# A local-attention, mixture-of-experts and gated-convolution kernel whose planner gets another table of due times and another table of engine choices

## The chip, the cores and the metric

The kernel runs on one core of a Trainium2 chip, as one launch. The metric is the device time of that launch in microseconds (us). Before the change it is 360.0 us, the median of 3 runs (359.75 to 361.68). The engines are named as the profile names them: PE (TensorE, matrix products and transposes), DVE (VectorE), ACT (ScalarE), POOL (GpSimd) and SP (SyncE, which issues the transfers).

## The reference, cut to what matters

B = 4 batches, H = 8 heads of D = 64, S = 576 positions, 512 model columns.

```
# 1. local attention, per batch and head
q_d, k_d, v_d = means over groups of 4 positions           # 144 positions
out_d    = softmax(q_d k_d^T / 8) v_d, repeated 4 times
scores   = q k^T / 8, and -1e9 where |i - j| >= 4
attn_out = out_d + softmax(scores) v                        # -> x: (B, S, 512)
# 2. mixture of 4 experts, head width 64, the best 2 per token
w = softmax over the 2 best of x w_gate
out = sum over e in best 2 of  w_e * (causal_softmax((x wq_e)(x wk_e)^T / 8) (x wv_e)) wo_e
# 3. gated causal convolution, 5 taps, on x = out
gate_pre[t] = sum_k conv_w[k] * x[t + k - 4];  gate = 1 / (1 + exp(-gate_pre))
result = (gate * (x w_val)) w_out
```

## The kernel before, in words

Batches follow each other, and the attention of the next batch is worked on beside the experts and the convolution of the present one. Heads go in pairs, 128 rows at a time.

*Attention.* Queries and keys arrive as 128 x 576 (two heads of 64 rows); the pair sums L941 and L948 make the pooled queries qd and keys kd, and L965 and L971 the pooled values vd. L1072 makes the pooled scores. The band scores are taken over query windows of 58 positions against 64 keys: L1131 puts the mask into a PSUM bank, L1137 adds the products. A softmax is a chain of pieces: the maximum L1002 (DVE), the factor L1008, the exponential, the sum, the small constant L1042 or L1044, the reciprocal L1048 (DVE) and the normalisation. The exponential has forms. L1013 is one ACT instruction per row group that also sums (a READ of its accumulator follows it in the trace); L1019 is the same without the sum, which L1033 or L1035 then does on DVE; L1024 and L1028 subtract on DVE and take all exponentials in one ACT instruction. The normalisation is L1057 on ACT (one instruction per row group, five for p, three for pd) or L1059 on DVE or POOL (one for all). PE transposes the weights (L1088 pooled, L1150 band), ACT or DVE copies them out of PSUM (L1095, L1157), PE multiplies with the values (L1106, L1172), and L1181 and L1189 make the 512 columns of x, which L793 and L810 split into a high and a low part.

*Weights.* They come as 8-byte numbers and are decoded by a chain of three ACT, POOL and DVE pieces with DVE's L858, L862 and L870; then they are split into high and low parts too. L891 multiplies the expert output weights with w_val. Products of split numbers are three matmuls, L1217 to L1219.

*Experts.* Projections by L1217 to L1219 (xh, xl with wqk; wvg makes values and gate), causal scores L1369, a softmax against a running maximum of scores (L1396, L1399, L1408 on ACT with sums), the gate's weight by L1509, transposes L1430 and L1447 (the fifth, last query tile of each pair of experts is L1447's), copies L785, and the products with the values L1541.

*Convolution and output.* wo and wv products again by L1217 to L1219; five taps, one with L1589 or L1596 on ACT and the others as L1603 on DVE, L1601 on POOL; L1608 is the tanh that stands for the sigmoid, L1614 the gate product, then the product with w_out, its scale L1635 or L1637, and the output's DMA L1641.

*What sets the order.* No instruction's place is written out by hand. The code builds `pieces`: some instructions of one engine with a cost, the buffers they read and write, and a due time. `order()` then plays the engines through in time: whenever an engine is free, of the pieces whose inputs are there and for which buffers are free (8 PSUM banks, two to six slots of each kind in SBUF) the one with the earliest due time is taken. The order so found is recorded, and the chip follows it on each engine, with semaphores between engines. Two tables feed it. `DUE` has one number for each piece (line 34 on), used in the line

```
p = Piece(engine, cost, late, (DUE[idx] if idx < len(DUE) else 0.0, idx), fn, k, size)
```

and `PICK` (line 254 on) has one digit for each choice that `pick(name, *options)` offers: which engine does a piece, or which form a softmax takes.

```
k = min(int(PICK[n]), len(options) - 1) if n < len(PICK) else 0
```

The rest of the file, below the tables, is this:

Of the kernel before, what the change touches and what calls it, by code (L numbers as in the profile page):

```python
# [34 lines left out]
    0.3, 0.5, 0.7, 3.85, 0.6, 0, 0.15, 3.6, 5.16, 4.91, 4.66, 0.9, 4.89, 0, 1.9, 5.41, 1, 0.5, 6.63,  # L35
    17.11, 6.13, 5.43, 6.16, 4.13, 5.94, 1.5, 2, 10.6, 25.96, 11.1, 6.27, 7.22, 7.34, 8.15, 18.43,
    20.51, 8.74, 10.69, 11.4, 11.74, 11.74, 13.08, 14.95, 16.34, 16.63, 11.2, 12.56, 13.48, 13.03,
    13.03, 15.15, 15.91, 17.43, 21.16, 22.44, 22.86, 23.49, 24.63, 27.11, 12.78, 14.43, 15.12, 15.59,
    15.58, 15.03, 15.03, 17.03, 18.05, 19.32, 19.54, 14.83, 15.43, 16.61, 15.9, 15.43, 15.43, 15.9,
    21.69, 22.83, 23.12, 24.4, 25.14, 25.74, 26.3, 27.38, 28.37, 29.43, 30.14, 27.38, 28.07, 31.01,  # L40
    31.52, 19.75, 21.9, 22.7, 23.34, 23.03, 22.5, 22.5, 23.03, 26.08, 29.26, 29.82, 22.3, 23.27, 23.74,
    26.08, 22.9, 22.9, 27.67, 28.27, 29.35, 29.66, 31.23, 31.97, 32.31, 32.87, 34.08, 34.96, 35.63,
    36.3, 34.08, 34.65, 35.24, 35.9, 17.61, 16.61, 30.21, 29.21, 31.71, 25.32, 26.64, 22.05, 23.27,
    21.39, 21.89, 29.71, 37.9, 36.9, 28.27, 29.02, 28.8, 29.44, 40.34, 42.55, 25.43, 26.88, 28.07,
    28.41, 28.41, 27.47, 27.47, 29.75, 30.82, 33.8, 34.26, 27.27, 27.87, 34.8, 28.34, 27.87, 27.87,
    28.34, 36.89, 37.7, 39.84, 29.95, 32.07, 32.78, 33.47, 33.47, 33.47, 36.74, 37.61, 37.92, 31.55,
    32.27, 32.61, 32.65, 35.38, 36.67, 37.52, 37.81, 39.55, 41.17, 40.65, 43.5, 45.55, 45.59, 41.88,
    42.94, 43.53, 45.32, 46.91, 47.84, 49.15, 49.64, 46.91, 46.91, 48.73, 50.53, 35.16, 36.73, 37.32,
    38.83, 37.66, 37.32, 37.32, 37.66, 42.32, 43.44, 43.96, 37.12, 37.72, 37.72, 37.72, 43.04, 43.64,
    44.5, 45.8, 46.06, 46.28, 48.1, 49.09, 49.61, 50.92, 51.93, 52.32, 52.95, 53.56, 51.93, 52.02,  # L50
    52.52, 53.15, 0, 3.77, 5.09, 4, 11.72, 12.4, 5.63, 14.81, 16, 3, 8.93, 9.43, 25.46, 31.3, 32.58,
    2.5, 8.32, 9.19, 18.11, 25.21, 26.79, 10.1, 16.43, 18.58, 1.6, 5.49, 4.8, 5.26, 5.03, 4.5, 3.5,
    10.69, 12.93, 12.05, 12.73, 13.71, 15.23, 16.11, 18.03, 5, 16.11, 20.41, 20.97, 21.19, 22.92, 24.05,
    25.57, 28.34, 27.15, 30.71, 28.71, 37.37, 36.81, 39.49, 40.24, 42.7, 44.9, 50.06, 48.86, 49.33,
    67.4, 71.57, 72.12, 72.74, 73.46, 74.01, 75.39, 78.04, 76.3, 79.23, 0, 80.02, 78.73, 0, 79.42,
    22.39, 30.95, 33.18, 28.21, 34.42, 37.79, 86.78, 92.73, 93.33, 93.14, 94.05, 97.11, 97.75, 98.07,
    98.12, 102.59, 103.62, 103.54, 104.39, 105.05, 106.89, 107.89, 108.63, 45.79, 53.97, 54.52, 54.88,
    55.81, 56.56, 58.16, 60.05, 62.54, 59.05, 63.22, 63.77, 63.99, 64.46, 65, 66.51, 67.46, 70.02,
    76.28, 80.78, 81.33, 82.34, 83.11, 83.9, 85.82, 86.81, 88.53, 58.91, 59.28, 59.64, 64.32, 65.01,
    64.91, 62.41, 62.87, 63.23, 63.6, 64.32, 64.59, 58.55, 60.88, 61.24, 63.96, 66.52, 64.8, 32.28,  # L60
    36.5, 53.1, 55.98, 57.01, 56.95, 53.65, 54.02, 54.38, 55.18, 57.27, 56.82, 68.36, 69.12, 65.52,
    69.46, 70.55, 71.62, 65.34, 66.33, 75.39, 75.72, 76.66, 77.25, 77.83, 78.14, 82.54, 89.2, 67.25,
    68.93, 69.29, 69.64, 70.23, 70.77, 66.8, 67.61, 68.48, 70.86, 72.41, 71.54, 73.13, 72.64, 73.44,
    74.58, 75.04, 75.95, 77.49, 64.68, 65.03, 65.39, 65.74, 66.78, 66.33, 68.81, 33.85, 37.07, 51.7,
    54.74, 57.26, 57.83, 55.41, 58.94, 57.02, 57.59, 71.31, 71.75, 72.2, 73, 73.81, 73.67, 74.33, 57.23,
    57.67, 58.11, 60.44, 61.77, 62.26, 61.55, 62.59, 61.11, 62.83, 55.54, 56.34, 56.78, 60, 60.67,
    60.67, 61.35, 5.93, 6.04, 73.79, 75.08, 75.61, 74.81, 76.22, 76.25, 76.91, 76.85, 78.27, 78.95,
    79.29, 79.56, 82.47, 79.56, 81.57, 79.56, 82.08, 79.56, 80.16, 85.84, 87.63, 87.08, 89.02, 92.07,
    91.37, 94.15, 95.99, 95.66, 79.51, 80.89, 81.95, 80.62, 82.37, 84.37, 85.62, 83.45, 86.36, 89.99,
    90.49, 90.76, 92.04, 90.76, 91.34, 90.76, 90.95, 91.57, 91.97, 92.6, 93.84, 93.47, 94.43, 95.73,  # L70
    95.49, 97.41, 102.01, 97.92, 87.91, 89.29, 90.25, 89.89, 90.81, 93.22, 93.98, 94.25, 94.84, 94.89,
    95.22, 96.2, 97, 99.88, 91.1, 92.4, 94.21, 94.15, 96.33, 97.81, 98.25, 98.52, 98.52, 98.52, 99.86,
    100.99, 103.14, 102.11, 91.98, 95.26, 93.61, 96.41, 98.17, 99.4, 98.92, 100.1, 100.58, 100.85,
    102.54, 103.76, 105.19, 105.82, 106.67, 109.23, 109.23, 109.77, 109, 110.83, 111.63, 112.46, 113.98,
    114.76, 115.1, 115.39, 116.83, 115.3, 116.32, 118.2, 118.93, 120.22, 118.7, 120.68, 121.72, 122.18,
    123.23, 124.36, 125.31, 125.6, 126.47, 125.58, 125.7, 129.07, 129.93, 129.93, 119.4, 122.92, 121.82,
    124.29, 125.23, 125.99, 125.51, 127.78, 128.09, 128.37, 128.81, 130.3, 131.05, 130.94, 132.65,
    135.21, 135.21, 135.89, 31.21, 26.47, 43.74, 59.55, 68.4, 42.02, 44.23, 33.89, 38.39, 36.4, 37.4,
    43.24, 63.64, 67.9, 45.03, 46.3, 47.08, 47.98, 51.16, 52.22, 46.68, 49.21, 49.81, 49.81, 49.81,
    50.04, 50.64, 52.75, 55.68, 56.92, 58.86, 48.81, 49.41, 49.41, 49.41, 50.44, 51.03, 53.45, 54.45,  # L80
    55.23, 56.16, 52.24, 53.85, 55.08, 55.62, 55.55, 55.55, 58.02, 58.85, 59.31, 54.37, 55.08, 57.54,
    55.52, 55.52, 59.19, 59.95, 60.25, 66.1, 67.2, 67.05, 75.39, 76.56, 76.73, 67.97, 69.72, 69.73,
    77.26, 78.27, 78.77, 79.71, 80.68, 78.27, 78.47, 79.15, 79.53, 61.6, 63.07, 63.78, 64.64, 64.12,
    63.67, 63.67, 64.12, 68.23, 68.72, 69.14, 63.47, 64.07, 64.62, 68.71, 64.07, 64.07, 70.15, 71.26,
    71.8, 72.09, 79, 80.09, 80.44, 81.01, 81.92, 82.68, 83.31, 85.14, 81.92, 82.04, 86.07, 88.5, 48.83,
    48.33, 53.33, 86, 79.55, 58.22, 60.04, 55.32, 55.88, 63.14, 62.64, 53.83, 98.62, 85.5, 67.23, 67.99,
    67.72, 68.63, 60.75, 77.43, 70, 71.89, 72.92, 74, 73.42, 73.42, 75.53, 76.16, 77.36, 71.1, 71.82,
    72.67, 72.16, 72.16, 75.32, 76.08, 76.36, 81.69, 83.86, 85.17, 86.55, 89.71, 90.96, 80.2, 81.24,
    81.88, 82.35, 82.71, 81.84, 81.84, 84.77, 85.69, 86.58, 87.33, 81.64, 82.3, 83.74, 82.77, 82.24,
    82.24, 82.77, 86.03, 87.54, 88.52, 90.46, 91.63, 92.88, 93.44, 94.88, 98.75, 100.61, 101.65, 96.09,  # L90
    98.07, 100.64, 101.02, 83.96, 86.68, 87.28, 87.28, 87.28, 88.1, 89.89, 90.56, 96.28, 96.78, 97.37,
    88.8, 89.4, 89.4, 89.4, 91.67, 92.37, 93.22, 94.99, 95.57, 96.28, 106.16, 106.9, 107.24, 109.63,
    110.64, 113.06, 114.61, 115.21, 110.64, 111.1, 111.73, 112.11, 95.84, 97.95, 98.56, 98.54, 99.14,
    98.54, 99.66, 98.54, 100.18, 98.54, 100.71, 101.35, 100.28, 100.64, 102.02, 103.38, 103.78, 97.59,
    99.92, 101.66, 100.51, 102.75, 100.51, 104, 104.83, 106.29, 100.99, 107.13, 108.72, 104.19, 104.65,
    109.4, 109.93, 110.5, 97.22, 99.12, 104.48, 99.71, 105.18, 99.71, 105.7, 99.71, 106.49, 99.71,
    107.69, 108.41, 105.44, 105.8, 109.07, 109.6, 110.17, 96.7, 98.76, 100.25, 99.35, 101.1, 99.35,
    101.62, 99.35, 102.35, 99.35, 103.14, 104.17, 102.6, 103.4, 104.85, 105.51, 106.1, 114.82, 115.53,
    115.89, 116.68, 117.31, 138.94, 111.17, 111.62, 111.98, 112.33, 113.49, 119.94, 112.69, 113.04,
    113.4, 115.18, 117.4, 117.89, 121.06, 122.57, 123.4, 126.24, 127.08, 139.44, 136.6, 139.13, 139.89,  # L100
    139.81, 140.95, 139.81, 141.87, 139.81, 142.53, 139.81, 143.12, 143.78, 147.01, 150.58, 151.5,
    152.1, 152.9, 139.57, 141.55, 144.5, 148.26, 148.89, 147.03, 149.72, 142.23, 150.85, 142.23, 151.9,
    152.56, 154.09, 154.63, 156.18, 156.79, 157.26, 122.12, 137.51, 138.19, 138.19, 140.49, 138.19,
# [1598 lines left out]
```

## Time and profile before

| what | value |
|---|---|
| median of 3 runs | 360.0 us (359.75 to 361.68) |
| the profiled execution's own time | 360.29 us |
| its span, first to last instruction | 358.6 us |
| mean granted clock of PE | 0.986 of full speed |
| busy: PE | 331.2 us (92%) |
| busy: DVE, ACT, POOL | 301.5, 257.8, 197.5 us (84%, 72%, 55%) |
| moved by DMA | 31.70 MB, mean 88 GB/s |

The span lies inside the profiled execution's time; 1.7 us are around it. Busy time is the time in which at least one instruction of the engine was under way. Shares are averages over the whole span, and the stages of this kernel differ, so the table of stretches further down says more than they do.

### The profile page before, as it was taken

The page shows a single profiled execution, that of the slowest core. Times are in us where ns is not written, and L with a number is a line of the kernel's source. Part 1 is how long each engine was busy: PE and PEld are TensorE (multiplying, and loading weights), DVE is VectorE, ACT ScalarE, POOL GpSimd, SP SyncE. Part 2 cuts the span into 40 slices and gives each one's busy share as a digit, 9 for nine tenths or more (in the row PEclk, how much of TensorE's full clock was granted, in tenths as well). Part 3 has the DMA queues.
Part 4 walks back from the last instruction along what each step waited for, and adds up shares of the span by engine and source line. Part 5 has one row for each costly group of instructions (what it writes and reads, how often), then busy time and mean ns, then how long its engine had stood idle before and what let it go on. Part 6 is the DMA issues. An engine that isn't in the chain of part 4 may idle for free.

```text
span 358.6 us, 11498 instructions
## 1 busy us (share of the span) xinstructions
PE 331.2 (92%) x4360; PEld 290.1 (81%) x4360; DVE 301.5 (84%) x922; ACT 257.8 (72%) x893; POOL 197.5 (55%) x309
## 2 busy tenths in 40 slices
PE   0598499898899999999999999999999999999996
PEld 0465379886587998999899898999989899987896
DVE  5789999989999799999998876867889678599481
ACT  2769546789997977888888799577964473588372
POOL 6697768569987243579877221663751024017151
PEclk9999679999999999999999999999999999999999
DMA  7879774437450224325512100022000000010012
GB/s 257 214 262 239 176 211 132 141 99 158 122 160 3 72 64 136 97 81 148 133 43 69 53 31 1 2 78 76 2 1 3 31 15 16 18 59 2 15 46 74
DMA packets 26279, 31.70 MB, mean 88 GB/s; under 512 B 2672, under 2 KB 18032, under 8 KB 26224
## 3 DMA queue, kind: packets, MB, share of 16 engines
q1 hardware_dynamic: 26224, 30.97, 30.2%
q8 instruction: 34, 0.56, 0.7%
q14 instruction: 21, 0.17, 0.2%
HBM read 26.24 MB, written 4.72 MB: 86 GB/s over the span
## 4 chain that ended last, share of the span: by engine, by line
PE 75%; DVE 16%; ACT 3%; POOL 1%; DMA 1%; issue 1%; SPq 0%; DVEq 0%; ACTq 0%; POOLq 0%
PE ps L1217 18%; PE ps L1218 15%; PE ps L1219 15%; PE ps L1541 6%; PE ps L1369 5%; PE ps L1430 3%; PE ps L1172 3%; DVE mx L1002 2%; PE ps L1150 2%; PE ps L1106 2%; PE ps L1137 2%; PE ps L1072 2%; DMA kt<-in_kT_dram 1%; PE ps L891 1%; DVE o L858 1%
## 5 line engine op out<-in xcount | busy, mean ns | idle before, releaser
L1408 ACT ACTIVATE pe<-ps,mmin 128x128 f32<-128x128 f32 (+4 forms) x80 | 42.1, 532 | 13.8 <-DVE mmin L1399 6.8
L1603 DVE SCALAR_TENSOR_TENSOR row<-ps,cw,row 128x256 f32<-128x256 f32 (+1 forms) x94 | 45.7, 510 | 5.4 <-POOL row L1601 2.7
L1601 POOL TENSOR_TENSOR row<-row,row 128x320 f32<-128x320 f32 (+1 forms) x34 | 28.5, 840 | 32.8 <-ACT row L1589 18.5
L1217 PE MATMUL ps<-gh,wout_h 128*128 128x256 f32 (+1 forms) x128 | 39.1, 306 | 0.0
L1217 PE MATMUL ps<-xh,wqk_h 128*128 128x256 f32 (+1 forms) x128 | 38.7, 302 | 0.4 <-ACT pd L1019 0.4
L1218 PE MATMUL ps<-gl,wout_h 128*128 128x256 f32 (+1 forms) x128 | 37.7, 295 | 0.0
L1218 PE MATMUL ps<-xl,wqk_h 128*128 128x256 f32 (+1 forms) x128 | 37.7, 295 | 0.0
L1219 PE MATMUL ps<-gh,wout_l 128*128 128x256 f32 (+1 forms) x128 | 37.7, 294 | 0.0
L1219 PE MATMUL ps<-xh,wqk_l 128*128 128x256 f32 (+1 forms) x128 | 37.5, 293 | 0.0
L1541 PE MATMUL ps<-mp,vE 128*64 128x320 f32 (+4 forms) x224 | 26.3, 367 | 0.3 <-ACT mp L785 0.3
L785 ACT COPY mp<-ps 128x384 f32<-128x384 f32 (+2 forms) x43 | 20.7, 508 | 7.7 <-PE ps L1430 5.6
L1002 DVE TENSOR_REDUCE mx<-ps 128x5 f32<-128x320 f32 (+1 forms) x48 | 23.7, 521 | 2.0 <-PE ps L1072 1.1
L1509 POOL TENSOR_SCALAR pe<-pe,rs,gw 128x128 f32<-128x128 f32 (+3 forms) x25 | 16.3, 659 | 16.5 <-DVE rs L1480 8.2
L1217 PEld LDWEIGHTS ps<-xh,wqk_h 128*128 128x128 f32 x128 | 24.1, 188 | 1.4 <-ACT pd L1019 0.6
L1217 PEld LDWEIGHTS ps<-gh,wout_h 128*128 128x128 f32 x128 | 24.1, 188 | 1.2 <-DVE sm L1033 0.2
L1217 PE MATMUL ps<-wvg_h,xh 128*128 128x260 f32 (+1 forms) x80 | 23.2, 290 | 1.5 <-DVE kl L810 1.5
L1218 PEld LDWEIGHTS ps<-xl,wqk_h 128*128 128x128 f32 x128 | 24.1, 188 | 0.1
L1218 PEld LDWEIGHTS ps<-gl,wout_h 128*128 128x128 f32 x128 | 24.1, 188 | 0.0
L1219 PEld LDWEIGHTS ps<-xh,wqk_l 128*128 128x128 f32 x128 | 24.1, 188 | 0.0
L1219 PEld LDWEIGHTS ps<-gh,wout_l 128*128 128x128 f32 x128 | 24.1, 188 | 0.0
L1541 PEld LDWEIGHTS ps<-mp,vE 128*64 128x64 f32 (+1 forms) x224 | 13.9, 135 | 11.8 <-issue 3.0
L1219 PE MATMUL ps<-wvg_h,xl 128*128 128x260 f32 (+1 forms) x80 | 22.8, 285 | 0.1
(229 smaller groups left out, 1211.0 us busy)
## 6 DMA issues: line engine op xcount, KB each, us to landing
kt<-in_kT_dram SPq DMA_DIRECT2D x16, 288.0 KB, 3.6
qt<-in_qT_dram SPq DMA_DIRECT2D x16, 288.0 KB, 4.1
v<-in_vx_dram SPq DMA_DIRECT2D x16, 288.0 KB, 5.0
vw<-in_vx_dram SPq DMA_DIRECT2D x16, 192.0 KB, 4.0
out_dram<-o SPq DMA_DIRECT2D x16, 160.0 KB, 1.9
raw<-in_w_val_dram SPq DMA_DIRECT2D x4, 512.0 KB, 5.5
vw<-in_vx_dram SPq DMA_DIRECT2D x16, 128.0 KB, 3.8
raw<-in_w_out_dram SPq DMA_DIRECT2D x4, 512.0 KB, 3.8
```

The lines of the kernel that those rows point to most:

```text
L785: (nc.scalar.copy if eng == "act" else ENG[eng].tensor_copy)(out(), src())
L1002: nc.vector.tensor_reduce(out=mx.t[:n, :g], in_=sv(), op=ALU.max, axis=AX.X)
L1172: nc.tensor.matmul(po.t[64 * h:64 * h + 64, t0:t0 + n], vw.t[k, 2 * m + c, 64 * h:64 * h + 64], pTs[c].t[k, (NC * h + m) * WQ2:(NC * h + m ...
L1217: nc.tensor.matmul(p, ah, bh, start=first, stop=False)
L1218: nc.tensor.matmul(p, ah, bl, start=False, stop=False)
L1219: nc.tensor.matmul(p, al, bh, start=False, stop=last)
L1369: nc.tensor.matmul(s.t[:, o:o + P * (t + 1)], a.t[r, P * t:P * t + P], z.t[r, :P * (t + 1)], start=(k == 0 and t == T[0]), stop=(k == 2 an ...
L1408: nc.scalar.activation(pe.t[:, off + c0:off + c1], s.t[:, o:o + c1 - c0], AF.Exp, bias=m.t[:, 0:1], scale=-1.0, accum_out=sums.t[:, a:a + ...
L1509: ENG[en].tensor_scalar(v, v, x, y, op0=ALU.mult, op1=ALU.mult)
L1541: nc.tensor.matmul(av.t[64 * e:64 * e + 64, z:n], vE.t[:kr, j, 2 * pr + e, :], pT.t[:kr, e, k0:k0 + n - z], start=(j == 0), stop=(j == Tl))
L1601: nc.gpsimd.tensor_add(g.t[:, :nn], g.t[:, :nn], g2.t[:, :nn])
L1603: nc.vector.scalar_tensor_tensor(g.t[:, :nn], x2.t[:, k:k + nn], cw.t[:, m, k:k + 1], g.t[:, :nn], op0=ALU.mult, op1=ALU.add)
```

## The change

The two tables get other numbers. All code below them is the same, line by line. Of the tables one line each stands for the rest (some 217 and 11 lines):

```diff
 DUE = (
-    0.3, 0.5, 0.7, 3.85, 0.6, 0, 0.15, 3.6, 5.16, 4.91, 4.66, 0.9, 4.89, 0, 1.9, 5.41, 1, 0.5, 6.63,
...
+    0.3, 1.5, 0.7, 5.45, 1.6, 0, 0.15, 3.85, 3.6, 5.2, 4.58, 0.5, 6.19, 2, 3.88, 4.83, 0, 1, 9.28, 4.5,
...
 PICK = (
-    "000010110142202100104210221000000112040200020020101011001051102120040211010112102132121101001000"
...
+    "011100000001230000010112021100012002032101000120010100100011231130040010001000000150042211001021"
...
```

What they do to the program is seen in the order of instructions on each engine. PE has 3142 instructions in both. DVE goes from 905 to 887, ACT from 572 to 567, POOL from 313 to 328. Over the whole program DVE has, for instance, 8 more copies L785 of mp and 7 more L1157, 6 fewer L1033 and 6 fewer L1603; ACT has L1013 of p 65 times instead of 35 and L1019 of p 45 times instead of 65; POOL has 6 more L1601 and 6 more L1509.

Names in the rows below are tile names with a buffer's number behind them: row is an SBUF slot of 348 columns, o one of 512 that holds a weight chunk, qt and kt queries and keys, ps a PSUM bank.

DVE near its start, before:

```order
L690 COPY band_171<-band_171 128x384
L793 CAST wvg_h<-o_163 128x260
L941 TENSOR_TENSOR row_102<-kt_73 128x288
L720 CAST identb<-ident 128x128
L810 TENSOR_TENSOR wvg_l<-o_163,wvg_h 128x260
L941 TENSOR_TENSOR row_105<-qt_71 128x288
L948 TENSOR_TENSOR kd_81<-row_102 128x144
L948 TENSOR_TENSOR qd_75<-row_105 128x3x48
L948 TENSOR_TENSOR qd_76<-row_106 128x3x48
L793 CAST wqk_h<-o_164 128x512
L810 TENSOR_TENSOR wqk_l<-o_164,wqk_h 128x512
```

and after:

```order
L941 TENSOR_TENSOR row_102<-qt_71 128x288
L690 COPY band_171<-band_171 128x384
L941 TENSOR_TENSOR row_103<-qt_72 128x288
L948 TENSOR_TENSOR qd_76<-row_103 128x3x48
L720 CAST identb<-ident 128x128
L941 TENSOR_TENSOR row_106<-kt_74 128x288
L948 TENSOR_TENSOR kd_82<-row_106 128x144
L793 CAST wvg_h<-o_163 128x260
L810 TENSOR_TENSOR wvg_l<-o_163,wvg_h 128x260
L810 TENSOR_TENSOR wvg_l<-o_164,wvg_h 128x260
L793 CAST wqk_h<-o_165 128x512
L810 TENSOR_TENSOR wqk_l<-o_165,wqk_h 128x512
```

The sums of the first qt (L941, L948) come ahead of the split of wvg, and two halves of wvg are split in a row instead of one ahead of the sums.

ACT in the first query tiles of batch 0, before:

```order
L1042 ACTIVATE sm_89<-sm_89 128x5
L1019 ACTIVATE p_93<-ps_65,mx_86 128x64 x5
L793 CAST xh_108<-row_103 128x348
L1057 ACTIVATE p_94<-p_94,sm_88 128x64 x5
L793 CAST xh_108<-row_106 128x228
L793 CAST wqk_h<-o_163 128x512
L1157 COPY pT_99<-ps_64 128x348
L1157 COPY pT_97<-ps_63 128x348
L1019 ACTIVATE pd_95<-ps_66,mx_84 128x3x48 x3
```

and after:

```order
L1013 ACTIVATE p_94,sm_89<-ps_64,mx_84 128x64 x5
L1013 ACTIVATE p_92,sm_88<-ps_63,mx_85 128x64 x5
L1181 COPY row_102<-ps_69 128x228
L1057 ACTIVATE p_94<-p_94,sm_89 128x64 x5
L1013 ACTIVATE p_93,sm_90<-ps_68,mx_87 128x64 x5
L793 CAST xh_108<-row_105 128x348
L1157 COPY pT_99<-ps_64 128x348
L1013 ACTIVATE p_94,sm_91<-ps_65,mx_86 128x64 x5
L1008 ACTIVATE mx_84<-mx_84 128x3
L1181 COPY row_103<-ps_66 128x228
```

L1019, which leaves the sum sm to DVE, has become L1013, which makes it on ACT; copies L1181 have come in between.

DVE just ahead of the transposes L1447 of batch 0's last query tile, before:

```order
L1509 TENSOR_SCALAR pe_135<-pe_135,rs_147,gw_130 128x512
L1603 SCALAR_TENSOR_TENSOR row_106<-ps_64,cw,row_106 128x256 x2
L1466 TENSOR_SCALAR es_153<-es_153 128x1
L1603 SCALAR_TENSOR_TENSOR row_106<-ps_64,cw,row_106 128x256
L1480 RECIPROCAL es_153<-es_153 128x1
L1603 SCALAR_TENSOR_TENSOR row_106<-ps_64,cw,row_106 128x256
L1603 SCALAR_TENSOR_TENSOR row_102<-ps_67,cw,row_102 128x256 x2
L1614 SCALAR_TENSOR_TENSOR row_106<-row_106,ps_68 128x256
L1603 SCALAR_TENSOR_TENSOR row_102<-ps_67,cw,row_102 128x256
L1603 SCALAR_TENSOR_TENSOR row_103<-ps_65,cw,row_103 128x256
L1603 SCALAR_TENSOR_TENSOR row_102<-ps_67,cw,row_102 128x256
L858 TENSOR_SCALAR o_163<-o_163 128x512
```

and after:

```order
L1466 TENSOR_SCALAR es_153<-es_153 128x1
L858 TENSOR_SCALAR o_164<-o_164 128x512
L1603 SCALAR_TENSOR_TENSOR row_106<-ps_68,cw,row_106 128x256
L1480 RECIPROCAL es_153<-es_153 128x1
L862 TENSOR_SCALAR o_164<-o_164 128x512
L1499 TENSOR_TENSOR rf_150<-es_153,ew_155 128x1
L1189 TENSOR_TENSOR row_105<-ps_66,od_101 128x348
L1614 SCALAR_TENSOR_TENSOR row_106<-row_106,ps_64 128x256
L1614 SCALAR_TENSOR_TENSOR row_103<-row_103,ps_69 128x256
L1614 SCALAR_TENSOR_TENSOR row_107<-row_107,ps_68 128x256
```

The taps L1603 that stand there before have been spread out or done earlier, and a chunk's decoding (L858, L862) and a column of x (L1189) have come ahead. Counted on each engine up to those transposes, DVE has 273 instructions before and 283 after, PE 905 and 949, ACT 233 and 263, POOL 135 and 126.

## Rows read from the trace of the kernel before

**Rows 1.** The page: PE's busy time, and the chain's shares by engine.
```profile
PE 331.2 (92%) x4360; PEld 290.1 (81%) x4360; DVE 301.5 (84%) x922; ACT 257.8 (72%) x893; POOL 197.5 (55%) x309
...
PE 75%; DVE 16%; ACT 3%; POOL 1%; DMA 1%; issue 1%; SPq 0%; DVEq 0%; ACTq 0%; POOLq 0%
```

**Rows 2.** Busy time (instructions) by stretch; PEclk, DMA share, GB/s at the end.
```profile
0.00:18.00 18.00, 6.14 (x71) 4.24 (x72) 12.20 (x36) 9.26 (x38) 11.65 (x39) 1.00 0.83 236
18.00:44.00 26.00, 18.91 (x362) 13.10 (x364) 24.77 (x57) 18.55 (x78) 21.00 (x28) 0.90 0.85 228
44.00:54.00 10.00, 10.00 (x195) 7.95 (x188) 9.48 (x23) 4.29 (x11) 6.66 (x11) 0.75 0.72 207
54.00:107.70 53.70, 49.02 (x702) 41.16 (x699) 51.19 (x161) 45.22 (x174) 43.01 (x62) 1.00 0.50 134
...
118.00:355.40 237.40, 236.81 (x2895) 215.19 (x2894) 193.70 (x624) 171.66 (x568) 108.14 (x165) 1.00 0.16 50
```

**Rows 3.** DVE's groups, 0 to 107.7 us: busy, mean ns, idle before them.
```profile
L1059 DVE TENSOR_TENSOR p<-p,sm 128x320 f32<-128x320 f32 x7 | 5.0, 715 | 0.1
L1033 DVE TENSOR_REDUCE sm<-p 128x5 f32<-128x320 f32 x10 | 4.7, 474 | 0.0
...
L1059 DVE TENSOR_TENSOR pd<-pd,sm 128x432 f32<-128x432 f32 x3 | 2.1, 703 | 0.0
L1157 DVE COPY pT<-ps 128x348 f32<-128x348 f32 x4 | 2.0, 506 | 0.3 <-ACT p L1013 0.3
L965 DVE TENSOR_TENSOR v<-v 112x768 f32<-112x768 f32 x2 | 1.9, 958 | 0.0
...
L941 DVE TENSOR_TENSOR row<-qt 128x288 f32<-128x288 f32 x3 | 1.6, 539 | 0.0
...
L810 DVE TENSOR_TENSOR wo_l<-o,wo_h 128x512 fp32r<-128x512 f32 x2 | 1.3, 662 | 0.0
...
L971 DVE TENSOR_TENSOR vd<-v 112x384 f32<-112x384 f32 x1 | 0.5, 546 | 0.0
```

**Rows 4.** PE's instructions in order of time: start, duration, what.
```profile
107.72 0.49 PE L1447 MATMUL ps<-ident,pe 64*64 64x64 f32 x10
...
156.37 0.59 PE L1150 MATMUL ps<-ident,p 64*128 64x64 f32 x12
156.89 0.33 PE L1131 MATMUL ps<-band,identb 64*64 64x320 bf16 x4
...
157.60 0.86 PE L1172 MATMUL ps<-pT,vw 64*64 64x58 f32 x40
158.40 0.41 PE L1217 MATMUL ps<-ah,wv_h 128*128 128x320 f32 x1
...
299.73 0.28 PE L1217 MATMUL ps<-wvg_h,xh 128*128 128x260 f32 x1
...
300.09 0.31 PE L1217 MATMUL ps<-ah,wv_h 128*128 128x320 f32 x1
...
300.52 0.31 PE L1217 MATMUL ps<-ah,wv_h 128*128 128x320 f32 x1
```

**Rows 5.** DVE and POOL in order of time, around 6.6 and 59 us.
```profile
6.58 0.30 DVE L948 TENSOR_TENSOR qd<-row 128x144 f32<-128x144 f32 x1
...
58.84 2.28 POOL L965 TENSOR_TENSOR v<-v 112x768 f32<-112x768 f32 x1
...
59.42 3.10 DVE L948 TENSOR_TENSOR qd<-row 128x144 f32<-128x144 f32 x1
```

**Rows 6.** ACT in order of time, around 24 and 29 us.
```profile
23.67 0.34 ACT L1013 ACTIVATE p<-ps,mx 128x64 f32<-128x64 f32 x1
23.87 0.23 ACT L1013 ACTIVATION_READ_ACCUMULATOR p<-ps,mx 128x1 f32 x1
23.96 0.34 ACT L1013 ACTIVATE p<-ps,mx 128x64 f32<-128x64 f32 x1
...
29.09 1.32 ACT L1057 ACTIVATE p<-p,sm 128x64 f32<-128x64 f32 x5
```

More of the change, by code (lines that the diff above doesn't have):

```diff
@@ L34 @@
 DUE = (
[217 rows of a table removed]
[217 rows of a table added]
 )
 PICK = (
-    "000010110142202100104210221000000112040200020020101011001051102120040211010112102132121101001000"
-    "101000210010011100001020010101010100010001010001101000010000001101010000100021111111121112000001"
-    "200201001000022201020101100001001110012102210212111000100010213115220002100010011101112002021101"
-    "410020001011212102120000112100002100110000000000000011000000011100210011210000010000001000111111"
-    "011111111101101101100011101111101202101010201200102200111100210112100120200010001010011011001020"
-    "100040021201001021222401000201001010000001111422010410100010121021212521000010110011010100110000"
-    "210000010001110101000000100011101021000010010101010110101110011010000000000111011111111210110002"
-    "200000011100121120010102011001000000101011011151121121002010110110111142041200020020011100101122"
-    "022031112001010010002142022101100111010120010021000121001110111000001110012010011110001001101001"
-    "010001011000000000000100101000101110110120210010010222001001210100001000001110221100101000000100"
-    "112000000111000000110000011000011110000000210001"
+    "011100000001230000010112021100012002032101000120010100100011231130040010001000000150042211001021"
+    "212000102110110000002121012101010100110000111000010000010000001111000000000100111111120211000001"
+    "001011102000101100222011001010001001003203201021101111010210012000120002102100100101110222121110"
+    "400100010010012202220000012000000100000110110110000000100000000001000011200000010000100011111000"
+    "100111001110010100101010010010101012110112122001002000101101201012011112010001011110110111322002"
+    "100132251111101121202220000010010111111010421420222020000000001121212221000110011001210001210111"
+    "110000200000010020000021000021000021101000101100010001110000110010010110011011001001210101111021"
+    "101011220000110011111211012211001010100101010120222130210011011100110140052211001011110100111152"
+    "130201102011010000012132101101011110001021110010101100010010001111110100002101110001000000110110"
+    "110100011101010010111011000010100000011022112010011100010022101001002110002000120100010000001110"
+    "110010002110010011010000210000211111200100000010"
 )
```

432 rows, old and new, of the table DUE are left out of this document.

## The prediction

> **What bounds the kernel now.** I read first the page's busy shares and its chain [rows 1]: PE is busy 92% of the span and holds 75% of the chain, DVE 16%. A share of the whole span says nothing about when, so the second view is the table of busy time by stage [rows 2]. From 118 us to 355.4 us PE is busy 236.81 of 237.40 us: there is no idle time there that an order could remove. Before 107.7 us PE is idle 11.86 + 7.09 + 0 + 4.68 = 23.6 us. In the same stretch DVE is busy 12.20 + 24.77 + 9.48 + 51.19 = 97.6 us; it is idle 5.80 us up to 18 us and only 1.23 + 0.52 + 2.51 = 4.3 us after that. So the early part goes at the pace of DVE, and the rest at the pace of PE. PE's clock was granted at a mean of 0.90 and 0.75 in 18 to 44 and 44 to 54 us, so a part of these was at the lower level (1.2 GHz), after PE had idled. It cost little: DVE is busy 9.48 of the 10 us at 0.75, so a faster PE would have waited for DVE.
>
> The end of the early part is a wait that the trace shows: the transposes of the last query tile of batch 0, L1447, at 107.72 us [rows 4]. Ahead of them stand most of DVE's early instructions; behind them PE runs on without a gap. I call them the milestone. The end of the kernel is the time of the milestone plus what PE still has to do then.
>
> **The change part by part.** Only the two tables move, so nothing is computed differently. PE has 3142 instructions in either program; DVE goes from 905 to 887, ACT from 572 to 567, POOL from 313 to 328. After 118 us DVE, ACT and POOL are busy 193.70, 171.66 and 108.14 of 237.40 us [rows 2], so what leaves DVE there is worth nothing by itself. The sum is made at the milestone.
>
> DVE ahead of the milestone: 273 instructions before, 283 after. By the means of their rows in the first 107.7 us [rows 3]: four normalisations L1059 of p fewer (4 x 0.715 = 2.86), three of pd (3 x 0.703 = 2.11), three sums L1033 (3 x 0.474 = 1.42), two splits of wo (2 x 0.662 = 1.32), together -7.7 us. Against it four copies L1157 (4 x 0.506 = 2.02), three pair sums L941 of q (3 x 0.539 = 1.62), two L971 (2 x 0.546 = 1.09) and one L965 (0.96), together +5.7. The rest is 12 more, of many lines; at DVE's mean of that stretch (97.6 us over 277 instructions, 0.35 [rows 2]) +4.2. Sum: +2.2 us of DVE ahead of the milestone. If I take for every instruction a short duration of its own kind (the lower quartile of the trace) the same difference is +2.9, because the removed ones are the ones that POOL lengthened.
>
> PE ahead of the milestone: three more triples of L1217 to L1219 with 256 columns and one with 320, and one more query pair's transposes L1150 and values product L1172 (two triples for wo go behind it, two for wv come before it, which cancels). A triple of 260 columns takes 300.09 - 299.73 = 0.36 us, one of 320 columns 300.52 - 300.09 = 0.43; the transposes take 156.89 - 156.37 = 0.52 and the product 158.40 - 157.60 = 0.80 [rows 4]. Sum: 3 x 0.36 + 0.43 + 0.52 + 0.80 = 2.8 us of PE work that is done in PE's early idle time instead of behind the milestone.
>
> So the milestone is 2.2 to 2.9 us later and the work behind it 2.8 us less: -0.6 to +0.1 us. I take -0.5, nearer to the means, as they are of this stretch.
>
> ACT ahead of the milestone gains more than any other: 15 more L1013 of p with their sums, 15 more L1057 of p and six of pd, ten fewer L1019. An L1013 with its sum is 23.96 - 23.67 = 0.29 us, of which the READ takes 23.96 - 23.87 = 0.09, so an L1019 is 0.20; an L1057 is 1.32 / 5 = 0.26 [rows 6]. 15 x 0.29 + 21 x 0.26 - 10 x 0.20 = 7.8, and the others take off 0.7: some 7 us. This is what pays for the fewer L1033 and L1059 on DVE. In 18 to 72 us or so ACT has room: it is idle 7.45 of the 26 us from 18 to 44, 5.71 of the next 10 and 8.48 of the 53.7 after that [rows 2], 21.6 in all. I cost it at nothing since 7 is a third of that; if the cover is gone it costs up to 7.
>
> POOL ahead of the milestone loses some 4 us (135 instructions to 126, at 43.01 / 62 = 0.69 for one of 54 to 107.7 us 6 us, at 21.00 / 28 = 0.75 nearly 7 [rows 2]; by each one's own kind 3.7). Its whole work rises by 15 instructions, 10 us, and all of that and more comes behind the milestone: 14 us more in a stretch where POOL has been idle 129 of 237 us. I cost that at nothing too; the cover is those 129 us.
>
> The start: the SP queue now loads the two qt first and the weights of values and gate later; DVE does the sums of q before the first split of wvg. The first product of the folded weights L891 comes out within a us of where it was, as the chain ahead of it gets less DVE work and a later load. The tail ends as before with PE's last triple, the scale L1635 on ACT and the output's DMA: nothing.
>
> Sum: profiled time 360.29 - 0.5 = 359.8. That run stands 0.3 above the median of the runs shown (360.0), so 359.5.
>
> **What the sum leaves out: waits between DVE and POOL.** DVE's L948 of qd at 59.42 us took 3.10 us where the same shape took 0.30 at 6.58; beside it POOL ran L965 from 58.84 for 2.28 us [rows 5]. That one instruction lost 2.8 us on the engine that sets the pace. Ahead of the milestone POOL has three L965 and four L971 before, two and two after. If the new order takes such a meeting away, its 2.8 us come off the milestone in full. If it makes a new one the same amount is added: three such splits of weights and pd normalisations come to POOL.
>
> The Trainium skill, page "SBUF — State Buffer", section "SBUF: two separate sides", says that VectorE and GpSimd share a port pair as an exclusive lock for the whole instruction when VectorE reads two SBUF operands and GpSimd reads SBUF, and the loser waits. The 3.10 us row agrees in kind: the instruction that starts second is the one that lasts long, though it ends 1.40 us after L965 has (62.52 against 61.12). By that rule the three removed long ones are worth more than the instruction counts say, which is rival A; without it the sum stays -0.5.
>
> **The rivals.** A, faster: meetings on DVE and POOL go away and DVE's gaps close. For it: 2.8 us in one row, 4.3 us of DVE idle after 18 us, fewer long POOL instructions. Against it: every other order has meetings of its own. One meeting and a third of the gaps is 2.8 + 1.4 = 4.2, so 359.5 - 4.2 = 355.3; own range 353.5 to 358.
>
> B, slower: ACT takes DVE's place as the pace of the early part. Its 7 us more fall where band scores turn into p: L1019 with L1033 on DVE becomes L1013 on ACT alone, and L1057 follows it on the same engine. It decides as soon as ACT's queue is late by more than its idle between two tiles; then PE's L1150 waits for ACT's L1057 and DVE goes idle. Against it: ACT's 21.6 idle us. Half of the 7 not hidden gives 363.0, all 366.5.
>
> C, slower: the 14 us more of POOL behind the milestone. POOL's conv taps and gate products stand in chains that PE's output product waits for; before, PE idles 0.59 us after 118 [rows 2]. Two to four instructions of POOL late, at its mean there of 108.14 / 165 = 0.66 us, is +1.3 to +2.6: 360.8 to 362.1.
>
> **How the numbers follow.** A measurement of this kernel tells about 0.5% (1.8 us) from no change: 358.2 to 361.8. My forecast has 0.38 (own range 358.2 to 361), A 0.37, B 0.15, C 0.10. The milestone sum carries the forecast; A nearly as much, since the early part is where 23.6 us of PE's idle lie and DVE's lengthened rows are its largest item. Faster: A, 0.37. Same: the forecast, 0.36 of its 0.38, and 0.03 of C: 0.39. Slower: B 0.15, the other 0.07 of C and 0.02 of the forecast: 0.24. The range leaves out A's lowest and B's worst: 354.5 to 364.
>
> **What would show it.** Right: L1447's first transposes of batch 0 at 109.5 to 111 us with PE busy within 1 us of the whole stretch from there to the end; DVE busy over 95% from 18 us to there. A: the milestone at or before 107 us, and no DVE row of over 2 us in the first 110. B: DVE idle over 6 us between 18 and 107 us, with ACT's L1057 or L1013 named as what PE or DVE waits for. C: PE idle over 2 us after 118 us, behind POOL. What would make me wrong in another way is a stall at the start over 2 us, or more time for PE at the lower clock where DVE does not cover it.

## The result

The changed kernel takes 357.12 us, the median of 4 runs (355.51 to 361.18); the kernel before, in the same rounds, 360.69. The ratio is 0.9881 with a 95% interval of 0.9839 to 0.9923: faster, by 4.3 us or 1.2%. Run again for the experiments, it came to 0.9884 (0.9830 to 0.9939). Four of the twelve executions of the changed kernel, and one of 89 of the kernel before, were some 3 to 6 us longer than the rest, most of them at a lower granted clock; the ratios leave those out, so a median beside them can be higher.

The forecast of no change (359.5) was not what happened. The time lies in the stated range (354.5 to 364), below the forecast's own (358.2 to 361) and inside that of rival A (355.3, own range 353.5 to 358). But the time was saved in another place than A's: behind the milestone, not ahead of it.

### The profile page after: what moved, and what is told of

It reads as the page before. It is cut to its first block, busy times and chain, and to the rows that moved or that the text cites. A ratio compares the mean times of both kernels' runs of the same rounds, so it can differ in the third digit from the quotient of the medians.

```text
span 355.2 us, 11527 instructions
## 1 busy us (share of the span) xinstructions
PE 331.5 (93%) x4360; PEld 290.3 (82%) x4360; DVE 301.0 (85%) x909; ACT 257.8 (73%) x923; POOL 205.5 (58%) x325
## 4 chain that ended last, share of the span: by engine, by line
PE 78%; DVE 14%; POOL 3%; ACT 2%; issue 2%; POOLq 0%; DVEq 0%
PE ps L1217 19%; PE ps L1218 17%; PE ps L1219 17%; PE ps L1541 7%; PE ps L1369 5%; PE ps L1430 3%; PE ps L1172 2%; DVE mx L1002 2%; PE ps L1137 1%; PE ps L1106 1%; PE ps L1150 1%; PE ps L1072 1%; PE ps L1088 1%; DVE sm L1044 1%; DVE row L1189 1%
## 5 line engine op out<-in xcount | busy, mean ns | idle before, releaser
L1601 POOL TENSOR_TENSOR row<-row,row 128x256 f32<-128x256 f32 (+1 forms) x40 | 32.1, 806 | 32.6 <-ACT row L1596 18.3
L1603 DVE SCALAR_TENSOR_TENSOR row<-ps,cw,row 128x320 f32<-128x320 f32 (+1 forms) x88 | 43.3, 514 | 6.2 <-ACT row L1589 4.3
L1509 POOL TENSOR_SCALAR pe<-pe,rs,gw 128x128 f32<-128x128 f32 (+3 forms) x31 | 21.1, 686 | 7.8 <-DVE mmin L1404 4.9
L1596 ACT ACTIVATE row<-ps,cw 128x256 f32<-128x256 f32 (+1 forms) x40 | 18.9, 506 | 5.1 <-PE ps L1219 2.6
```

The lines of the kernel that those rows point to most:

```text
L1509: ENG[en].tensor_scalar(v, v, x, y, op0=ALU.mult, op1=ALU.mult)
L1596: nc.scalar.activation(g2.t[:, :nn], x2.t[:, k:k + nn], AF.Copy, scale=cw.t[:, m, k:k + 1])
L1601: nc.gpsimd.tensor_add(g.t[:, :nn], g.t[:, :nn], g2.t[:, :nn])
L1603: nc.vector.scalar_tensor_tensor(g.t[:, :nn], x2.t[:, k:k + nn], cw.t[:, m, k:k + 1], g.t[:, :nn], op0=ALU.mult, op1=ALU.add)
```

## The profile after

The chain's shares on the page of the changed kernel, which answer to [rows 1]; its span is 355.2 us.

```profile
PE 78%; DVE 14%; POOL 3%; ACT 2%; issue 2%; POOLq 0%; DVEq 0%
```

The chain holds 78% PE and 14% DVE, as against 75% and 16%.

The stretches up to 107.7 us as in [rows 2], with the same columns:

```profile
0.00:18.00 18.00, 6.55 (x89) 4.72 (x90) 13.88 (x37) 10.26 (x40) 10.70 (x36) 0.92 0.94 263
18.00:44.00 26.00, 20.89 (x391) 14.63 (x392) 24.24 (x59) 21.74 (x96) 19.54 (x26) 0.76 0.93 232
44.00:54.00 10.00, 10.00 (x170) 8.07 (x165) 9.52 (x26) 7.59 (x37) 7.32 (x12) 0.91 0.57 164
54.00:107.70 53.70, 50.32 (x746) 42.71 (x747) 52.24 (x167) 44.64 (x171) 40.06 (x54) 0.94 0.49 125
```

Up to 107.7 us DVE is busy 13.88 + 24.24 + 9.52 + 52.24 = 99.88 us where it was 97.64: 2.24 us more, the size that the sum had forecast. It is idle 7.82 us instead of 10.06: 1.68 less up to 18 us, 0.56 less after that. ACT is busy 84.23 us there instead of 77.32, the 7 us of the prediction. PE's granted clock is lower than before in three of the four stretches.

The milestone, which answers to the first row of [rows 4]:

```profile
107.73 0.47 PE L1447 MATMUL ps<-ident,pe 64*64 64x64 f32 x10
```

and the stretch from the milestone to the end of PE's last matmul, in the columns of [rows 2], of before, of the changed kernel, and of E10 (an experiment below, the changed kernel with PE work added behind the milestone):

```profile
107.72:355.35 247.63, 247.09 (x3043) 223.65 (x3042) 203.88 (x649) 180.05 (x595) 115.18 (x173) 1.00 0.16 48
...
107.73:351.97 244.24, 243.69 (x2984) 220.15 (x2980) 201.13 (x626) 173.14 (x584) 127.87 (x198) 1.00 0.17 50
...
107.46:354.48 247.02, 246.48 (x3144) 222.98 (x3140) 201.41 (x626) 173.06 (x584) 127.70 (x198) 1.00 0.17 49
```

The milestone is at 107.73 us; it was at 107.72. PE's last matmul ends at 351.97, before at 355.35. So the whole 3.4 us of difference lie behind the milestone. There PE has 59 matmuls less, is busy 3.40 us less, and is idle as long, 0.54 and 0.55 us. Of this 2.8 us were counted; the other 0.6 is spread over PE's spacing in 244 us, and I can't assign it.

The length of this stretch is firm. It is 244.20 to 244.53 us in the ten traces that have the changed kernel's order there, with spans from 355.2 to 362.2 us, and 247.35 in E1, which has the order of the kernel before there. The place of the milestone is not firm: E9, E11 and E12, whose times can't be told from the changed kernel's, have it at 108.90, 109.45 and 108.75. One trace against another tells little ahead of it. By the ratio the whole change is 4.3 us; with 3.4 of them behind the milestone, the milestone itself came 0.9 us earlier, give or take 1.5 (from the 95% interval of the ratio, here and further down).

As a ledger the pair of traces looks simple: DVE had 2.2 us more to do ahead of the milestone and lost 2.2 us less idle time. But E10 is the same program up to the milestone, and its trace has this:

```profile
0.00:107.46 107.46, 88.58 (x1382) 70.08 (x1384) 98.02 (x285) 84.31 (x340) 77.20 (x128) 0.92 0.70 178
```

Here DVE is busy 98.02 us and idle 9.44, so 0.4 more and 0.6 less than before. Busy time holds the waits inside an instruction, and differs between executions of the same instructions by as much as the term in question. So traces and ratio show that the milestone did not become later; they do not show whether shorter gaps or shorter instructions made room for the work that DVE got.

The question is what each term is worth by itself. The start, DVE and PE of the kernel before (start, duration, what, idle time before it and its releaser):

```profile
4.24 0.46 DVE L941 TENSOR_TENSOR row<-kt 128x288 f32<-128x288 f32 x1 [0.46 <-DMA kt<-in_kT_dram]
5.51 0.46 DVE L720 CAST identb<-ident 128x128 bf16<-128x128 f32 x1 [0.81 <-POOL ident masks.py:199]
...
7.62 0.31 DVE L948 TENSOR_TENSOR qd<-row 128x144 f32<-128x144 f32 x1 [0.73 <-POOL row L941]
8.66 0.43 DVE L793 CAST wqk_h<-o 128x512 fp32r<-128x512 f32 x1 [0.73 <-DMA o<-in_wqk_dram]
...
10.72 1.12 DVE L1002 TENSOR_REDUCE mx<-ps 128x3 f32<-128x432 f32 x2 [0.81 <-PE ps L1072]
...
6.93 0.74 PE L1072 MATMUL ps<-kd,qd 64*64 64x144 f32 x4 [6.93 <-DVE qd L948]
9.42 1.00 PE L1072 MATMUL ps<-kd,qd 64*64 64x144 f32 x12 [1.75 <-POOL kd L948]
```

and of the changed kernel:

```profile
3.77 0.48 DVE L941 TENSOR_TENSOR row<-qt 128x288 f32<-128x288 f32 x1 [0.51 <-DMA qt<-in_qT_dram]
4.70 0.38 DVE L690 COPY band<-band 128x384 bf16<-128x384 bf16 x1 [0.44 <-POOL band L685]
...
6.58 0.68 DVE L720 CAST identb<-ident 128x128 bf16<-128x128 f32 x1 [0.70 <-POOL ident masks.py:199]
...
10.27 1.12 DVE L1002 TENSOR_REDUCE mx<-ps 128x3 f32<-128x432 f32 x2
...
7.96 1.87 PE L1072 MATMUL ps<-kd,qd 64*64 64x144 f32 x24 [7.96 <-POOL kd L948]
```

With qt and kt first in SP's queue, DVE's first sum starts at 3.77. All scores L1072 follow each other from 7.96; before, the first four products came earlier, at 6.93, but PE then waited 1.75 us, until 9.42, for POOL's kd. DVE's idle times of 0.73, 0.73 and 0.81 us (for POOL's pair sum, a weight and the scores) are gone; 0.44 us for the band has come in, and the wait for the identity is 0.70 instead of 0.81.

DVE beside POOL, in the changed kernel; the first row is the quiet case, and the last is of the kernel before, the POOL instruction behind the L965 of [rows 5]:

```profile
14.23 0.16 DVE L1044 TENSOR_SCALAR sm<-sm 128x3 f32<-128x3 f32 x1
...
28.55 1.24 DVE L1044 TENSOR_SCALAR sm<-sm 128x5 f32<-128x5 f32 x1
...
58.50 1.89 POOL L965 TENSOR_TENSOR v<-v 112x768 f32<-112x768 f32 x1
...
58.72 1.71 DVE L1044 TENSOR_SCALAR sm<-sm 128x3 f32<-128x3 f32 x1
...
68.95 1.22 DVE L1044 TENSOR_SCALAR sm<-sm 128x5 f32<-128x5 f32 x1
...
61.08 1.28 POOL L810 TENSOR_TENSOR wout_l<-o,wout_h 128x512 fp32r<-128x512 f32 x1
```

Rival A looked for a DVE row of over 2 us; there is none now, where [rows 5] had one of 3.10. But L1044, an addition on 3 to 5 columns that takes 0.16 us undisturbed, took 1.24, 1.71 and 1.22 us: the one at 58.72 ends at 60.43, with POOL's L965 (58.50 + 1.89 = 60.39). The Trainium skill, page "SBUF — State Buffer", section "SBUF: two separate sides", has it that whichever of the two starts first holds the shared ports for its whole instruction and the other is blocked, where VectorE's instruction is in a 2-port mode or reads two SBUF operands while GpSimd's reads SBUF. These rows agree, and show that a small loser pays as much as a large one; whether L1044 ran in a 2-port mode no run shows. Not every meeting costs: the L1044 at 243.09 took 0.15 us while POOL ran L1509 from 242.16 for 1.32. The 3.10 us of [rows 5] go further: L948 had waited since 59.42, POOL's L965 ended at 61.12, and still POOL's next instruction, L810, ran first (61.08 + 1.28 = 62.36). L948 ended at 62.52, so it lost to two instructions in a row.

## The experiments

Each was compared with the kernel before in five rounds; against the changed kernel (0.9881 and 0.9884 in its two sets) a difference of some 0.006, or 2 us, is at the edge of what these intervals tell. The trace of each stands beside its ratio; ahead of the milestone it is one draw, as said above. For E1 to E3 and E12 the order was not planned anew: the recorded order of a kernel was replayed, with its slots, and moved where the edit says. E12 shows that a replay by itself costs nothing that can be told.

**E1, the start of the changed kernel in the kernel before.**

```diff
-order and choices of before
+pieces that the changed kernel records in its first 24 us: its order and choices
+all others: order and choices of before
```

> The kernel before, with the order and the engine choices of the changed kernel for everything that the changed kernel records in its first 24 us or so, and before's own order for the rest. Theory (the gain was made at the start): DVE has 2.2 us more work done at 25 us, as in the changed kernel, nothing later gives it back, and the time is 357.5 to 358.5, 2 to 3 us under the kernel before. Rival (the gain comes from the engine choices and the order after 25 us): no change, 359.5 to 361.5.

Ratio 1.0038 (1.0010 to 1.0067): slower than before, so neither theory held. Two stretches of before, of the changed kernel and of E1, one after the other:

```profile
0.00:25.00 25.00, 12.45 (x204) 8.42 (x208) 17.98 (x49) 13.70 (x55) 18.21 (x46) 1.00 0.85 253
25.00:107.70 82.70, 71.63 (x1129) 58.02 (x1119) 79.67 (x226) 63.61 (x244) 64.11 (x92) 0.94 0.60 159
```

```profile
0.00:25.00 25.00, 12.86 (x255) 9.28 (x255) 20.17 (x53) 15.84 (x65) 14.71 (x42) 0.86 0.87 247
25.00:107.70 82.70, 74.90 (x1130) 60.86 (x1130) 79.72 (x233) 68.40 (x275) 62.92 (x86) 0.90 0.62 157
```

```profile
0.00:25.00 25.00, 11.91 (x255) 8.34 (x255) 20.06 (x53) 16.71 (x68) 15.03 (x43) 0.93 0.92 262
25.00:107.70 82.70, 72.17 (x1066) 57.25 (x1068) 78.18 (x222) 62.23 (x237) 62.33 (x90) 0.92 0.62 156
...
107.63 0.49 PE L1447 MATMUL ps<-ident,pe 64*64 64x64 f32 x10
```

In the first 25 us E1 has all of the gain, 20.06 us of DVE work as against 17.98. Behind that its DVE is idle 82.70 - 78.18 = 4.5 us where before's is idle 3.0 and the changed kernel's 3.0 (E10's, with the changed kernel's order, 4.2). The milestone is where it was, at 107.63, in a trace of the fastest of E1's executions. So the start by itself was worth nothing in before's own order.

**E2, the reverse**: before's first 24 us in the changed kernel.

> The reverse: the changed kernel with before's order and engine choices for the first 24 us or so. Theory (the start): some 2 us slower than the changed kernel, 358.5 to 360. Rival (the rest): no slower than the changed kernel, 356 to 358.

1.0054 (1.0018 to 1.0089), some 6 us over the changed kernel, far more than the start's 2.2. In its trace the milestone is at 114.81 us and the stretch behind it is 244.25, as in the changed kernel: all of it is lost ahead of the milestone.

**E3**: the changed kernel's order up to 106 us, before's after that.

> The kernel before, with the changed kernel's order and engine choices for all that it records in its first 106 us, and before's own order behind that. Theory (all of the gain lies ahead of the first transposes L1447, and what follows is PE's work without a gap): as fast as the changed kernel, 356.5 to 358. Rival (the late part, where POOL has 14 us more work, gave or took something): off by over 1.5 us from the changed kernel, to either side.

1.0083 (1.0044 to 1.0122). In its trace (an execution of 369.72 us) PE is idle 3.1 us behind the milestone, 1.72 of it at 160.42 us for ACT, where it is idle 0.5 to 0.6 in the traces of all other kernels here. The rival's words fit, but neither parent has these waits, so they come with the seam, the place where two orders are joined, and E3 says nothing on POOL's late work. What the three show together is that the parts of an order do not add. That an order continues the state which its own beginning leaves is my reading of it, and not shown.

**E4, three tiny additions taken off DVE.**

```diff
-            if tiny == "act":
+            if tiny == "act" or key in ("020", "11d", "111"):
```

> The changed kernel, with three additions of the small constant (L1044, 28.55, 58.72 and 68.95 us, which took 1.24, 1.71 and 1.22 us on DVE beside POOL, where the shortest took 0.15) done by ACT at the same place of the order. Theory A (a wait of DVE for POOL ahead of the milestone is paid in full): 3.7 us off the early part, some 353 to 354. Rival (the next instruction on DVE takes the wait over, or another chain sets the pace): no change, 356.5 to 358.

0.9954 (0.9927 to 0.9982): not faster, but 2.6 us slower than the changed kernel, give or take 1.8; theory A fell. DVE and POOL of E4 near 90 us:

```profile
87.52 0.22 DVE L1396 TENSOR_REDUCE mmin<-ps 128x1 f32<-128x64 f32 x1 [0.64 <-PE ps L1369]
...
89.06 1.47 DVE L1509 TENSOR_SCALAR pe<-pe,rs,gw 128x128 f32<-128x128 f32 x1
...
90.85 1.54 DVE L948 TENSOR_TENSOR kd<-row 128x144 f32<-128x144 f32 x1
92.31 0.48 DVE L1002 TENSOR_REDUCE mx<-ps 128x5 f32<-128x320 f32 x1
...
89.17 1.27 POOL L810 TENSOR_TENSOR wout_l<-o,wout_h 128x512 fp32r<-128x512 f32 x1
90.41 1.81 POOL L965 TENSOR_TENSOR v<-v 112x768 f32<-112x768 f32 x1
```

and DVE and POOL of the changed kernel at the same instructions:

```profile
88.91 0.23 DVE L1396 TENSOR_REDUCE mmin<-ps 128x1 f32<-128x64 f32 x1 [0.63 <-PE ps L1369]
...
90.44 0.35 DVE L1509 TENSOR_SCALAR pe<-pe,rs,gw 128x128 f32<-128x128 f32 x1
...
91.10 0.98 DVE L948 TENSOR_TENSOR kd<-row 128x144 f32<-128x144 f32 x1
92.01 0.48 DVE L1002 TENSOR_REDUCE mx<-ps 128x5 f32<-128x320 f32 x1
...
90.57 1.35 POOL L810 TENSOR_TENSOR wout_l<-o,wout_h 128x512 fp32r<-128x512 f32 x1
```

Of the 3.7 us, 1.39 are left at the first row; at the last DVE row E4 is 0.30 us behind. In between L1509 took 1.47 instead of 0.35 and L948 1.54 instead of 0.98. L1509 starts 0.11 us ahead of POOL's L810 in E4 and 0.13 ahead in the changed kernel, and waits for it in one and not in the other; L948 waits in both, in E4 for the longer L965. The waits removed came back as others. E4's milestone is at 108.04 us and the stretch behind it 244.21, so the trace shows no gain; why the mean is slower it does not show.

**E5, the changed kernel again**, as reference.

> The changed kernel once more, in the same rounds as the next three, as their reference. Expected 356 to 358.5, 0.985 to 0.995 of the kernel before.

0.9884 (0.9830 to 0.9939).

**E6, DVE held up at the start.**

```diff
     for p in order:
         p.fn()
+        if p.due[1] == 31:
+            for _ in range(9):
+                nc.vector.memset(idle, 0.0)
```

> The changed kernel, with nine MEMSETs of a spare tile (128x240, some 2.2 us in all) on DVE right behind the second L948 of qd, at 5.5 us. Nothing else moves. Theory (the time that DVE lost at the start before the change, and loses no longer, is worth its full size): as much later at L1447's first transposes of batch 0 and at the end, +1.7 to +2.5 us against the changed kernel. Rival (the early part has other waits that take up a shift at the start, as in the transplanted start): +0 to +0.8.

0.9940 (0.9904 to 0.9977), 2.0 us over the changed kernel by the ratios. DVE's row of it, and the milestone:

```profile
6.07 2.88 DVE L1661 MEMSET idle<- 128x240 f32 x8
...
108.40 0.47 PE L1447 MATMUL ps<-ident,pe 64*64 64x64 f32 x10
```

Eight of the nine took 2.88 us at once, so some 3.2 in all and not 2.2. The milestone is 0.67 us later in this trace, the span 0.7. The ratios leave the price anywhere from nothing to its full size (2.0 us, give or take 2.4), so E6 does not decide between the two.

**E7, the same at 47 us** (`p.due[1] == 223`).

> The changed kernel, with the same nine MEMSETs (some 2.2 us) on DVE at about 47 us, in the middle of the early part. Theory (DVE sets the pace up to 107.7 us): +1.7 to +2.5 us at the end. Rival (in 60 to 80 us PE is busy without a gap, and waits of DVE for POOL shift to other places): under +1.

0.9989 (0.9955 to 1.0023): 3.8 us over the changed kernel, give or take 2.3.

```profile
46.77 3.26 DVE L1661 MEMSET idle<- 128x240 f32 x9
...
111.27 0.47 PE L1447 MATMUL ps<-ident,pe 64*64 64x64 f32 x10
```

3.26 us put in, the milestone 3.54 us later, the span 3.5. Here DVE's time has a price, and ratio and trace fit its full size; the rival's "under +1" is out.

**E8, PE's work early twice** and **E10, late twice.**

```diff
     for p in order:
         p.fn()
+        if p.due[1] in (83, 116, 192, 225):      # E10: (1998, 2031, 2107, 2140)
+            p.fn()
```

> The changed kernel, with the first four values products L1172 of batch 0 (24 to 50 us, 0.8 us each at full clock) made twice, 3.2 us more of PE work in the early part, the results the same. Theory (PE's work ahead of the milestone lies beside DVE's and costs nothing): +0 to +0.8 us. Rival (PE is on the path there too, since some of it runs at the lower clock): +2 to +4.

> The changed kernel, with four values products L1172 of batch 2 and 3 (200 to 248 us, 0.8 us each) made twice: 3.2 us more of PE work behind the milestone. Theory (behind the milestone PE's work is the time, so 2.8 us of it moved ahead are worth 2.8): +2.8 to +3.6 us against the changed kernel. Rival (other engines set the pace in part): under +1.5.

E8: 0.9931 (0.9891 to 0.9971), +1.7 us, span 356.8 (+1.6). E10: 0.9940 (0.9899 to 0.9982), +2.0 us, span 357.7 (+2.5). The ratios, give or take 2 us and more, decide neither. The trace decides E10, since its work lies in the firm stretch: from the milestone to the end it is 247.02 us instead of 244.24, and PE is busy 246.48 instead of 243.69. So the four products were 2.8 us of work, not 3.2, and behind the milestone they were paid in full. E8's milestone is at 109.09 us, among those of E9, E11 and E12, and the stretch behind it is 244.53; so whether PE's work ahead of the milestone has a price is not shown.

**E9, PE filled where it waits at 82 us** (`p.due[1] in (715,)`, called twice).

> The changed kernel, with one values product L1172 of batch 1 (80.9 us, 0.84 us) made twice, so that PE has work in the 1.28 us in which it waits for DVE's L1189 at 82 us; after that wait its clock is granted at the lower level from about 84 to 90 us. Theory (the lower level there follows the idle time, and costs time in the runs where it lasts to 104 us): the granted clock stays at 1.00 from 84 to 90, and the mean is 0.5 to 1.5 us under the changed kernel. Rival (DVE sets the pace there in any case, as 4.3 to 5 us of its 5 us are busy): the clock may stay up, and the time is the changed kernel's, plus up to 0.8.

0.9897 (0.9860 to 0.9935): no difference that can be told. PE's wait and a stretch of the changed kernel, two stretches of E9, and one of E10, which up to there is the changed kernel once more; the clock is the third column from the end:

```profile
83.29 0.99 PE L1088 MATMUL ps<-ident,pd 48*112 48x48 f32 x17 [1.28 <-DVE row L1189]
...
85.00:90.00 5.00, 4.83 (x70) 3.53 (x74) 4.30 (x18) 4.09 (x19) 4.75 (x8) 0.50 0.48 108
```

```profile
85.00:90.00 5.00, 4.03 (x90) 2.91 (x90) 4.93 (x19) 4.10 (x21) 4.83 (x7) 1.00 0.73 148
90.00:95.00 5.00, 3.71 (x28) 2.56 (x25) 4.96 (x12) 4.33 (x14) 4.92 (x7) 0.71 0.56 148
```

```profile
85.00:90.00 5.00, 4.98 (x76) 3.69 (x76) 4.53 (x16) 5.00 (x23) 4.75 (x9) 0.52 0.59 128
```

The clock of 85 to 90 us went from 0.50 to 1.00, as the theory had it, and fell in the next stretch instead, to 0.71. But in E10 PE waits only 0.33 and 0.72 us between 80 and 85 us, in E9 still 0.58, and E10's clock is 0.52 all the same. So it is not shown that the fill kept the clock up. DVE is busy 4.3 to 5.0 us of each 5. The result fits the rival, that DVE decides there; the 0.5 to 1.5 us of the theory are too little for these ratios to rule out.

**E11, ACT held up.** Ten copies of 128x240 between 26 and 58 us.

> The changed kernel, with ten copies of a spare tile (128x240) on ACT, two behind each of five of its softmax steps between 26 and 58 us, some 3 us in all, and one MEMSET of that tile on POOL at the very start. Theory (ACT had room for the 7 us it got): +0 to +0.8 us. Rival B of the prediction (ACT is at the edge of setting the pace): +2 to +3.

0.9894 (0.9857 to 0.9931), +0.4 us, give or take 2. The ten copies took 0.39 to 0.47 us each, 4.1 in all, so ACT has room for most of it. DVE is idle 3.7 us from 18 to 107.7 us in the changed kernel, where rival B needed over 6. B did not come.

**E12, late constants later**, the version that might have beaten both.

```diff
 POOL
-L734 to L746 (causal, later, tri, L)
 L678 MEMSET band ...
 ...
 L793 CAST wvg_h
+L734 to L746
```

> The changed kernel, with POOL's nine instructions for the late constants (L734 to L746, 0.78 to 2.6 us) moved behind the split of wvg (L793, 7.86 us), into the 4 us in which POOL then waits; two small ACT copies that read them (L1516) go behind L1008. The band and the identity are then there some 1.8 us earlier; DVE waited for them 0.44 and 0.70 us. Theory (time of DVE and of the first scores at the start is worth something at the end): L1072 starts 0.8 to 1.5 us earlier, and the time is 0.5 to 1.5 us under the changed kernel. Rival (a shift at the start is taken up by later waits, as the transplanted start was): within 0.5 us of the changed kernel.

0.9888 (0.9833 to 0.9944): no better than the changed kernel that can be told. DVE, POOL and PE of its start:

```profile
5.49 0.23 DVE L720 CAST identb<-ident 128x128 bf16<-128x128 f32 x1 [0.20 <-POOL ident masks.py:199]
7.22 0.46 DVE L941 TENSOR_TENSOR row<-kt 128x288 f32<-128x288 f32 x1 [1.51 <-DMA kt<-in_kT_dram]
...
6.51 0.67 POOL L941 TENSOR_TENSOR row<-kt 128x288 f32<-128x288 f32 x1 [1.06 <-DMA kt<-in_kT_dram]
...
8.02 1.87 PE L1072 MATMUL ps<-kd,qd 64*64 64x144 f32 x24 [8.02 <-POOL kd L948]
```

The identity is there 1.1 us earlier (5.49 for 6.58), and DVE then waits 1.51 us for kt. L1072 starts at 8.02, where it was without the edit (7.96). What sets these scores is the arrival of kt, for which POOL waits until 6.51 and DVE until 7.22.

## Why the prediction was wrong where it was

- The counts were right, and so was the split at the milestone. ACT has 7 us more ahead of it (6.91 measured), hidden as far as E11 can tell; POOL has 12.7 us more behind it (127.87 against 115.18, where 14 were forecast), also hidden, as PE is idle 0.5 us there in both kernels. Rivals B and C did not come.
- The step that failed is "the milestone is 2.2 to 2.9 us later". It priced each counted instruction of DVE at its mean and took DVE's gaps and waits as given, the start ("nothing") among them. The milestone was at 107.73 us, and at 107.46 in E10, instead of 109.5 to 111. That is some 2.2 of the 2.9 us between the -0.5 of the sum and the -3.4 of the traces.
- The other 0.6 is the size of PE's term: 2.8 us counted, 3.4 measured behind the milestone. The mechanism of this term was right, for the part behind the milestone: E10 put 2.8 us of PE's work back there and the stretch became 2.8 us longer. That the work was free ahead of the milestone is argued, not shown (E8).
- What took in DVE's 2.2 us stays open. In one trace DVE's gaps are 2.24 us shorter, 1.68 of it before 18 us; in the other of the same order 0.6 in all, 1.23 shorter before 18 us and longer after. E7 shows that DVE's time in the middle has a price; E6 can't tell it at the start; E1 shows that the start alone is worth nothing under before's order; E12 that a part of the start hides only the next wait.
- Rival A had the right sign and nearly the size, but not the place. Its 4.2 us were to come off the milestone, at or before 107 us, and the milestone did not move. No DVE row of over 2 us is left in the first 110 us, as A had it: the longest wait for POOL went, and smaller ones took their place. E4 shows why betting on one of them fails. That its number came closer than the forecast's is luck.

## What to carry to other kernels

Find the point where the pace goes over from one engine to another, and read each trace in two parts there. Behind it PE was never idle by more than 0.6 us in these two kernels, so work moved ahead of that point came off the time in full. Ahead of it two executions of the same program differed by as much as the change, so one trace against another priced nothing. A count of instructions at their mean durations need not become a delay: here 2.2 us of it on the engine that sets the pace there delayed nothing, since gaps and waits are not fixed. Do not price one wait between two engines that meet all the time at its own length; taking three away here gave nothing. And do not expect parts of a tuned order to keep their worth in another order.

## What the runs showed of the hardware

An instruction on 3 columns took 1.71 us on DVE beside POOL, over ten times its 0.16. A DVE instruction that waits for POOL can lose to POOL's next instruction too: 3.10 us for L948 through L965 and L810 in the kernel before, where 0.30 was its quiet time. PE's granted clock was 0.50, the lower of its two levels (1.2 GHz), for 85 to 90 us after PE had waited 1.28 us at 82 us. In E9, with that wait at 0.58, it was 1.00, and in E10, with waits of 0.33 and 0.72, it was 0.52; so the runs do not show what made it fall. The time of E9 did not differ by more than can be told.
